# Attention with two expert layers on one core: weights scaled in their own step, one preparation step per block product, sums in PSUM

## The chip, the cores and the metric

The kernel runs on one core of a Trainium2 chip. The metric is the device time of one execution, in microseconds; lower is better. Five engines matter here: PE (TensorE, matrix products into PSUM), DVE (VectorE), ACT (ScalarE), POOL (GpSimd) and SP, whose queue issues all transfers. Each engine works through its own instructions in order and waits for the others by semaphores.

## What is computed

```
scores = (q @ k^T) / 8, causal mask, softmax          # 2 batches, 12 heads, 448 tokens, 64 wide
x = attention output, 896 tokens x 768
h = x @ w_in; g = h where h>=1, 0 where h<=-1, else (h+1)^2/4; y = g @ w_out       # 768 -> 2048 -> 768
xn = y / rms(y) * rms_g
out = (silu(xn @ w_gate) * (xn @ w_val)) @ w_out2                                   # 768 -> 1536 -> 768
```

The weights arrive as 64-bit floats, two 32-bit words each.

## The kernel before

The tokens are held transposed, in two halves h of 448 columns, so that every matrix product is 128x128 weights times 128x448 tokens. Each operand is kept as a high part and a low part (fp32r), and each product is the sum of three: high·high, high·low, low·high.

**Weights.** Each weight block, 128x768, is one item of a list. Its 768 KB are loaded into one of three stage buffers (`w_load`), and then steps turn the two words of a number into an fp32 value: `w_scale` (ACT, L167) multiplies the upper word, `w_low` (L169) calls it and has POOL make the low bits (L174), `w_high` (DVE, L185) joins both, and `parts` splits the value: ACT casts the high part (L193), POOL subtracts for the low part (L194). As soon as a stage buffer is read, `w_next` issues the next item's transfer into it. All these steps stand in one list; `w_run(n)` emits the next n of them at the place of the program where it is called, `w_pace(x)` emits 4x on average, `w_need(n)` all up to item n, and `w_cap` says how far they may run ahead. Every engine's order is thus the order in which the program emits, and nothing reorders it. `w_low(n)` scales item n and then item n+1 too:

```
    def w_low(n):
        w_scale(n)
        w_scale(n + 1)
```

**Stages.** Attention (to about 98 us), then the first expert layer (L363: w_in; L606 in `out1`: w_out, half h=0, then h=1), then the second. In `out1(1)` the sixteen blocks n are 18 products each; the four plain w_gate items and the first pair are prepared beside them. Then the sum of squares (`rms_sum`), the spread of the scale over the partitions (`rms_spread`, PE L665), and the token sums that a Strassen-like scheme needs: `normalise`, `mix` and `mix_late` make T1 to T4 and B22 out of the two halves (DVE L669, L734 to L743, ACT L674, POOL L675), beside the products `head` and `tail` of the first four gate blocks.

**Rounds.** For each of 12 blocks f a pair of items, w_gate[f] and w_val[f], is turned into sums of their 384-column halves, S1 to S4 (`combine_a`, `combine_b`: DVE L438 to L443), and block products `p1` to `p7` of nine matmuls each (L700) give the two outputs: five products per round for f<4, where `head` and `tail` did two, and seven from f=4 on. Pair f+1 is prepared in round f. Results leave PSUM by ACT copies (L769, L778, L790) or DVE additions (L710), and Silu (L797, L812) and products (L713) follow in SBUF. A pair takes ten steps, emitted at 1.44 or 2 per product.

**Last stage.** `out2` (L852): twelve w_out2 items, plain steps again, and 432 matmuls in two halves; ACT copies, and the output leaves.

## Time and profile before

| | us |
|---|---|
| median of 3 runs | 704.04 (703.42 to 704.18) |
| the profiled execution, its own time | 704.87 |
| its span in the profile | 703.2 |
| PE busy | 622.9 (89%) |
| ACT, DVE, POOL busy | 323.7, 315.5, 300.4 |
| mean granted TensorE clock | 0.937 |

PE's busy time counts matmuls at whatever clock was granted, so a stretch at half clock looks busy. The page's forty slices show PE full until the second third of the run and between six and nine tenths from there to the last weights; no other engine passes half of its time after attention. The views to read are therefore the busy time by stretch, the waits, and the timeline of the stretches where PE has gaps.

### The profile page before, as it was taken

The numbers are of one execution on the slowest core, as the hardware profiler recorded it, in microseconds if no ns is written. First come the engines' busy times: TensorE is split into PE (matmuls) and PEld (weight loads), VectorE is DVE, ScalarE is ACT, GpSimd is POOL, SyncE is SP. The second block draws the span as 40 slices with busy tenths as digits, with TensorE's granted clock in tenths as the row PEclk, the third lists the DMA queues.
The fourth block names the chain that finished last, engine by engine and source line by source line (L and its number), as shares of the span: only waits on it lengthen the run. The fifth ranks groups of instructions, "written<-read, shape, count | busy, mean of one in ns | idle before, by whom it ended". The sixth has DMA issues, their size and how long they took to land.

```text
span 703.2 us, 8626 instructions
## 1 busy us (share of the span) xinstructions
PE 622.9 (89%) x3236; PEld 529.3 (75%) x3236; DVE 315.5 (45%) x573; ACT 323.7 (46%) x636; POOL 300.4 (43%) x241
## 2 busy tenths in 40 slices
PE   7999999999999999998696576978788997888998
PEld 4666678999998997987584455867676876766997
DVE  5777742432333334233448554534444464425210
ACT  6887863666665443322235333333334443443311
POOL 3434422656554444225328444544444563554000
PEclk9999999999999999999888777888888899999999
DMA  8324210444543422012120222222222223441202
GB/s 291 126 86 132 99 59 1 135 170 149 176 155 115 134 91 89 1 46 90 57 79 0 90 90 89 90 89 90 90 90 79 102 89 106 162 137 45 80 1 79
DMA packets 17274, 68.19 MB, mean 97 GB/s; under 512 B 2064, under 2 KB 6672, under 8 KB 17232
## 3 DMA queue, kind: packets, MB, share of 16 engines
q1 hardware_dynamic: 17232, 67.64, 28.7%
q8 instruction: 25, 0.41, 0.2%
q14 instruction: 17, 0.14, 0.1%
HBM read 64.88 MB, written 2.75 MB: 96 GB/s over the span
## 4 chain that ended last, share of the span: by engine, by line
PE 47%; POOL 14%; issue 13%; DMA 11%; DVE 10%; ACT 5%; POOLq 0%; SPq 0%; ACTq 0%; DVEq 0%
PE ps L363 17%; POOL ar L194 10%; PE ps L852 8%; DMA af<-in_w_gate 8%; PE ps L269 5%; PE ps L606 4%; PE ps L300 4%; PE ps L700 4%; POOL af L174 4%; PE ps L348 3%; DVE af L185 3%; DMA af<-in_w_out 2%; ACT af L167 1%; PE ps L334 1%; DVE af L442 1%
## 5 line engine op out<-in xcount | busy, mean ns | idle before, releaser
L194 POOL TENSOR_TENSOR ar<-af,ar 128x768 fp32r<-128x768 f32 (+1 forms) x92 | 164.3, 1791 | 236.5 <-ACT ar L193 229.2
L700 PE MATMUL ps<-ar 128*128 128x448 f32 x756 | 186.0, 410 | 49.9 <-DVE af L710 20.2
L700 PEld LDWEIGHTS ps<-ar 128*128 128x128 f32 x756 | 159.9, 215 | 75.0 <-DVE af L710 23.2
L606 PE MATMUL ps<-ar 128*128 128x448 f32 x576 | 127.0, 380 | 10.7 <-ACT ar L566 7.2
L606 PEld LDWEIGHTS ps<-ar 128*128 128x128 f32 x576 | 111.6, 195 | 25.3 <-ACT ar L566 9.4
L363 PE MATMUL ps<-ar 128*128 128x448 f32 x576 | 117.6, 366 | 0.0
L167 ACT ACTIVATE af<-af 128x768 f32<-128x768 f32 x66 | 59.8, 907 | 120.7 <-DMA af<-in_w_gate 78.3
L363 PEld LDWEIGHTS ps<-ar 128*128 128x128 f32 x576 | 108.0, 188 | 8.6
L193 ACT CAST ar<-af 128x768 fp32r<-128x768 f32 (+1 forms) x92 | 74.4, 818 | 84.2 <-DVE af L185 76.9
L185 DVE SCALAR_TENSOR_TENSOR af<-af 128x768 int32<-128x768 int32 x72 | 68.6, 955 | 74.3 <-POOL af L174 74.1
L852 PE MATMUL ps<-ar 128*128 128x448 f32 x432 | 93.2, 374 | 9.4 <-DVE ar L836 5.1
L852 PEld LDWEIGHTS ps<-ar 128*128 128x128 f32 x432 | 81.8, 191 | 20.8 <-DVE ar L836 7.6
L174 POOL TENSOR_SCALAR af<-af 128x768 int32<-128x768 uint8 x72 | 67.8, 942 | 14.7 <-DMA af<-in_w_out 5.2
L567 DVE TENSOR_TENSOR ar<-af,ar 128x448 fp32r<-128x448 f32 x32 | 28.4, 893 | 73.8 <-ACT ar L566 73.8
L284 ACT ACTIVATE af<-ps,nm 112x336 f32<-112x336 f32 (+2 forms) x96 | 46.9, 500 | 7.1 <-DVE nm L276 7.1
L710 DVE TENSOR_TENSOR af<-ps,af 128x448 f32<-128x448 f32 x44 | 26.7, 621 | 50.8 <-PE ps L700 50.6
L276 DVE CUSTOM_DVE_ANT_0 ps<-ps,af 112x336 f32<-112x336 f32 (+2 forms) x96 | 41.6, 473 | 13.7 <-PE ps L269 12.6
L836 DVE TENSOR_TENSOR ar<-af,ar 128x448 fp32r<-128x448 f32 x24 | 20.7, 874 | 57.7 <-ACT ar L835 57.7
L713 DVE TENSOR_TENSOR af<-af 128x448 f32<-128x448 f32 x24 | 23.6, 985 | 40.7 <-ACT af L812 32.3
L269 PE MATMUL ps<-af 64*112 64x448 f32 (+3 forms) x192 | 35.5, 448 | 4.9 <-DVE af L247 4.7
L675 POOL TENSOR_TENSOR ar<-af,ar 128x448 fp32r<-128x448 f32 x18 | 23.8, 1339 | 27.5 <-ACT ar L674 27.4
L566 ACT CAST ar<-af 128x448 fp32r<-128x448 f32 x32 | 17.7, 563 | 29.8 <-PE ps L606 29.8
(72 smaller groups left out, 476.8 us busy)
## 6 DMA issues: line engine op xcount, KB each, us to landing
af<-in_w_out SPq DMA_DIRECT2D x28, 768.0 KB, 4.3
af<-in_w_in SPq DMA_DIRECT2D x16, 768.0 KB, 4.3
af<-in_w_gate SPq DMA_DIRECT2D x16, 768.0 KB, 4.2
af<-in_w_val SPq DMA_DIRECT2D x12, 768.0 KB, 4.3
af<-in_kT SPq DMA_DIRECT2D x12, 224.0 KB, 2.7
af<-in_qT SPq DMA_DIRECT2D x12, 224.0 KB, 3.3
af<-in_v SPq DMA_DIRECT2D x12, 224.0 KB, 2.6
out_T<-af SPq DMA_DIRECT2D x12, 224.0 KB, 1.9
```

Of the source, the lines that this page charges most:

```text
L167: nc.scalar.activation(c, c, ACTF.Prelu, scale=2.0 ** -112, alpha=-2.0 ** 32)
L174: nc.gpsimd.tensor_scalar(out=words(n, 0, I32), in0=b, scalar1=1.0 / 32, scalar2=-31.0 / 64, op0=ALU.mult, op1=ALU.add)
L185: nc.vector.scalar_tensor_tensor(out=t if raw is None else raw.bitcast(I32), in0=words(n, 1, I32), scalar=3, in1=t, op0=ALU.logical_shift_ ...
L193: nc.scalar.copy(hi, src)
L194: nc.gpsimd.tensor_tensor(out=lo, in0=src, in1=b32(hi), op=ALU.subtract)
L269: nc.tensor.matmul(bs[j][:C, o:o + (c + 1) * C], lhsT=q[r, c * C:(c + 1) * C], rhs=k[r, :(c + 1) * C], start=True, stop=True, skip_group_c ...
L276: nc.vector.tensor_tensor_reduce(out=t, in0=t, in1=mask[:C, S - (c + 1) * C:], scale=-1.0, scalar=3e38, op0=ALU.add, op1=ALU.min, accum_ou ...
L284: nc.scalar.activation(Pn[:C, j, poff[c]:poff[c] + w], sbank[n][j][:C, o:o + w], ACTF.Exp, bias=nm[:C, j, c:c + 1], scale=-1.0, accum_out= ...
L363: nc.tensor.matmul(out, lhsT=w[:, a, k * P:(k + 1) * P], rhs=x[:, c, k], start=(k == 0 and n == 0), stop=(k == NK - 1 and n == 2))
L606: nc.tensor.matmul(ybs[dm][:, :S], lhsT=w[:, a, dm * P:(dm + 1) * P], rhs=t[:, c], start=(n == 0 and i == 0), stop=(n == NM - 1 and i == 2))
L700: nc.tensor.matmul(b[:, :S], lhsT=w(a, k), rhs=x[:, c, k], start=first and k == 0 and i == 0, stop=(k == HK - 1 and i == 2), skip_group_ch ...
L852: nc.tensor.matmul(obs[dm][:, :S], lhsT=w[:, a, dm * P:(dm + 1) * P], rhs=t[:, c], start=(kk == 0 and i == 0), stop=(kk == NF - 1 and i == 2))
```

## The change

- `w_low(n)` scales the next item only where that item is marked early: w_in, w_out, and w_out2 after its first. The w_gate and w_val items are scaled in their own `w_low`.
- A pair now has seven steps: `gate_low`; `gate_high` (which also does the val item's `w_low`); `val_high` (with the parts of the gate block); `sums_a`; `sums_b`; `parts_a`; `parts_b`. One is emitted per product from f=4 on (`w_run(1)`), seven among five products for f<4; the second pair's first two are emitted among `head` and `tail`.
- From the second pair on, the val half v1 and the sums s1, s2 lie in PSUM banks 5, 6 and 7; the low parts of s1 and s2 are then made by DVE.
- `squares` scales by rms_g on ACT instead of DVE; for h=1 the sum of squares is made by DVE, in PSUM.
- The normalised tokens, one token sum (t2) and the results z and y of `p4` and `p3` lie in PSUM; T2 and B22 get their low part from DVE, T1, T3, T4 from POOL. `mix_a` begins before `tail(0)`.
- All PSUM banks are fixed by number.

The core of the diff:

```diff
     def w_low(n):
         w_scale(n)
-        w_scale(n + 1)
+        if n + 1 < len(items) and items[n + 1][2]:
+            w_scale(n + 1)
...
     def pair_steps(n, f):
         bl = block(f)
...
+        g1, g2 = rawg[:, :KP], rawg[:, KP:]
+        v1, s1, s2 = (bank(i)[:, :KP] for i in (5, 6, 7)) if f else (rawv[:, :KP], sraw[:, 2], sraw[:, 3])
+        v2, s3, s4 = rawv[:, KP:], sraw[:, 0], sraw[:, 1]
+        s12 = pst[:, 6:8, :KP] if f else sraw[:, 2:4]
...
+        def gate_low():
+            w_low(n)
+        def gate_high():
+            w_high(n, rawg)
+            w_next(n)
+            w_low(n + 1)
+        def val_high():
             if f >= NA:
                 parts(bl[:, 0, 5:7], bl[:, 1, 5:7], rawg.rearrange("p (a b) -> p a b", a=2))
+            w_high(n + 1, v1, v2)
+            w_next(n + 1)
+        def sums_a():
+            tt(s1, v1, v2, ALU.add)
+            tt(s3, g1, v1, ALU.subtract)
+        def sums_b():
+            tt(s2, s1, g1, ALU.subtract)
+            tt(s4, g2, s2, ALU.subtract)
+            parts(bl[:, 0, 4], bl[:, 1, 4], v2)
+        def parts_a():
+            nc.scalar.copy(bl[:, 0, 0:2], s12)
+            tt(bl[:, 1, 0:2], s12, b32(bl[:, 0, 0:2]), ALU.subtract)
+        def parts_b():
+            parts(bl[:, 0, 2:4], bl[:, 1, 2:4], sraw[:, 0:2])
...
+        return [gate_low], [gate_high, val_high, sums_a, sums_b, parts_a, parts_b]
...
+        def mix_a(i):
+            x0 = XF[0]
+            normalise(1, i, XA[i])
+            normalise(1, i + HK, XB[i])
+            xt = XF[1][i]
+            sub(xt, XA[i], x0[i])
+            sub(t2, XB[i], xt)
+            operand(T1, i, xt)
+            operand(T2, i, t2, nc.vector)
+        def mix_b(i):
+            x0 = XF[0]
+            sub(x0[i], t2, x0[i])
+            sub(x0[i + HK], x0[i + HK], t2)
+            operand(T3, i, x0[i])
+            operand(B22, i, XB[i], nc.vector)
+            operand(T4, i, x0[i + HK])
...
+        yb = [bank(f % 2) for f in range(NF)]
+        zb = [bank(2 + f % 2) for f in range(NF)]
+        cb = bank(4)
...
         def p4(f):
+            z = zb[f][:, :S]
             product(zb[f], op(f, A22), T4, first=False)
-            add(TMP[f][0], zb.pop(f), TMP[f][0])
-            mul(A[f][0], A[f][0], TMP[f][0])
+            add(z, zb[f], TMP[f][0])
+            mul(A[f][0], z, A[f][0])
...
             if f < NA:
-                run = [(p6, f), (p4, f - 1), (p7, f), (p5, f), (p3, f - 1)]
+                m = f < 2
+                run = [(p4, f - 1, 2), (p6, f, 2), (p7, f, 1), (p5, f, int(m)), (p3, f - 1, 2 - m)]
+            else:
+                run = [(p1, f, 1), (p4, f - 1, 1), (p6, f, 1), (p3, f - 1, 1), (p7, f, 1), (p5, f, 1), (p2, f, 1)]
+            for p, g, n in run:
                 if g >= 0:
                     p(g)
-                w_pace(0.36 if f >= NA else 0.5)
+                w_run(n if f < NF - 1 else 2)
```

The instructions, one by one, stand now as follows at three places. First ACT in one round from f=4 on. Before (L769, L778, L790: copies of `p1`, `p6`, `p5`; L812, L797: Silu; L167: scale; L193: parts):

```order
L769 COPY af<-ps 128x448
L167 ACTIVATE af<-af 128x768
L193 CAST ar<-af 128x768
L778 COPY af<-ps 128x448
L167 ACTIVATE af<-af 128x768
L812 ACTIVATE af<-ps 128x448
L790 COPY af<-ps 128x448
L193 CAST ar<-af 128x384
L797 ACTIVATE af<-af 128x448
L193 CAST ar<-af 128x768 x2
```

Now (L805, L812, L823: the copies; L842, L829: Silu; L475: the high part of s1 and s2; L200: the other parts):

```order
L805 COPY af<-ps 128x448
L167 ACTIVATE af<-af 128x768 x2
L812 COPY af<-ps 128x448
L200 CAST ar<-af 128x768
L842 ACTIVATE ps<-ps 128x448
L200 CAST ar<-af 128x384
L823 COPY af<-ps 128x448
L475 CAST ar<-ps 128x768
L829 ACTIVATE af<-af 128x448
L200 CAST ar<-af 128x768
```

Both scales now stand together behind the copy of `p1`; before, one scale (of the next pair's gate item) stood ahead of Silu and of the copy of `p5`.

Second, POOL in one round. Before (L174: low bits; L194: low parts):

```order
L174 TENSOR_SCALAR af<-af 128x768
L194 TENSOR_TENSOR ar<-af,ar 128x768
L174 TENSOR_SCALAR af<-af 128x768
L194 TENSOR_TENSOR ar<-af,ar 128x384
L194 TENSOR_TENSOR ar<-af,ar 128x768 x2
L174 TENSOR_SCALAR af<-af 128x768
```

Now (L175 and L201 are the same lines):

```order
L175 TENSOR_SCALAR af<-af 128x768 x2
L201 TENSOR_TENSOR ar<-af,ar 128x768
L201 TENSOR_TENSOR ar<-af,ar 128x384
L201 TENSOR_TENSOR ar<-af,ar 128x768
L175 TENSOR_SCALAR af<-af 128x768 x2
```

The gate's parts moved behind the second low bits, and one of the two 128x768 low parts at the end went to DVE.

Third, ACT in the last stage, two items. Before (L835: the tokens' high part, L193: the weights' high part, L167: scale):

```order
L835 CAST ar<-af 128x448
L193 CAST ar<-af 128x768
L167 ACTIVATE af<-af 128x768
L835 CAST ar<-af 128x448
L193 CAST ar<-af 128x768
L167 ACTIVATE af<-af 128x768
```

Now (L867 is the tokens' line):

```order
L167 ACTIVATE af<-af 128x768
L200 CAST ar<-af 128x768
L867 CAST ar<-af 128x448
L167 ACTIVATE af<-af 128x768
L200 CAST ar<-af 128x768
L867 CAST ar<-af 128x448
```

The tokens' cast moved from behind a scale and ahead of a high part to behind the high part.

## Rows read from the trace of the kernel before

**Rows 1.** Busy times by stretch: span, PE, PEld, DVE, ACT, POOL (instructions), clock, DMA share, GB/s

```profile
360.00:405.00 45.00, 27.96 (x107) 23.42 (x107) 28.70 (x39) 18.37 (x34) 24.07 (x19) 0.76 0.10 35
405.00:451.00 46.00, 36.41 (x136) 31.16 (x137) 23.51 (x35) 13.32 (x20) 21.61 (x17) 0.78 0.28 91
451.00:574.00 123.00, 102.88 (x444) 90.40 (x443) 59.33 (x79) 47.33 (x76) 60.66 (x43) 0.89 0.26 88
```

**Rows 2.** Waits, whole run: who waited for whom, us in total, times, longest us

```profile
...
ACT af L167 <- DMA af<-in_w_gate: 78.3, 15, 9.5
...
PE ps L700 <- DVE af L710: 20.2, 7, 4.2
...
```

**Rows 3.** Timeline, L606 stage to spread: start us, us, instruction, count, [idle before <-releaser]

```profile
...
269.49 0.88 ACT L167 ACTIVATE af<-af 128x768 f32<-128x768 f32 x1 [5.25 <-DMA af<-in_w_gate]
...
274.09 23.26 PE L606 MATMUL ps<-ar 128*128 128x448 f32 x104 [1.49 <-DVE ar L567]
...
306.12 3.96 PE L606 MATMUL ps<-ar 128*128 128x448 f32 x18
309.50 0.88 ACT L167 ACTIVATE af<-af 128x768 f32<-128x768 f32 x1 [6.22 <-DMA af<-in_w_gate]
...
346.56 0.88 ACT L167 ACTIVATE af<-af 128x768 f32<-128x768 f32 x1 [6.75 <-DMA af<-in_w_val]
...
347.94 10.22 PE L606 MATMUL ps<-ar 128*128 128x448 f32 x36 [3.90 <-ACT ar L566]
...
364.18 1.89 PE L665 MATMUL ps<-ident,rr 112*128 112x112 f32 x8
```

**Rows 4.** Timeline, the rounds of the second expert layer

```profile
471.16 15.24 PE L700 MATMUL ps<-ar 128*128 128x448 f32 x63 [4.20 <-DVE af L710]
...
555.82 0.91 ACT L167 ACTIVATE af<-af 128x768 f32<-128x768 f32 x1 [3.06 <-DMA af<-in_w_gate]
...
576.72 2.10 PE L700 MATMUL ps<-ar 128*128 128x448 f32 x9 [1.00 <-DVE af L710]
```

**Rows 5.** Timeline, last weights' low parts on POOL and PE's last stretch

```profile
578.62 1.83 POOL L194 TENSOR_TENSOR ar<-af,ar 128x768 fp32r<-128x768 f32 x1 [0.23 <-ACT ar L193]
...
593.66 1.87 POOL L194 TENSOR_TENSOR ar<-af,ar 128x768 fp32r<-128x768 f32 x1 [2.00 <-ACT ar L193]
...
641.04 1.88 POOL L194 TENSOR_TENSOR ar<-af,ar 128x768 fp32r<-128x768 f32 x1 [2.34 <-ACT ar L193]
...
648.54 51.14 PE L852 MATMUL ps<-ar 128*128 128x448 f32 x251 [1.17 <-DVE ar L836]
```

**Rows 6.** Groups by shape: line, operation, count, busy us, mean ns, idle before

```profile
L710 DVE TENSOR_TENSOR af<-ps,af 128x448 f32<-128x448 f32 x44 | 26.7, 621 | 50.8 <-PE ps L700 50.6
...
L641 DVE TENSOR_TENSOR af<-af 128x448 f32<-128x448 f32 x1 | 0.6, 624 | 0.0
...
L438 DVE TENSOR_TENSOR af<-af 128x384 f32<-128x384 f32 x12 | 6.7, 558 | 0.4
...
L442 DVE TENSOR_TENSOR af<-af 128x384 f32<-128x384 f32 x12 | 13.2, 1099 | 0.0
...
L185 DVE SCALAR_TENSOR_TENSOR af<-af 128x768 int32<-128x768 int32 x26 | 24.7, 954 | 14.5 <-POOL af L174 14.5
...
L167 ACT ACTIVATE af<-af 128x768 f32<-128x768 f32 x26 | 23.6, 910 | 64.1 <-DMA af<-in_w_gate 56.2 <-DMA af<-in_w_out 7.9
...
L193 ACT CAST ar<-af 128x768 fp32r<-128x768 f32 x35 | 28.4, 833 | 39.1 <-DVE af L185 31.8 <-DVE af L442 6.9 <-DVE af L443 0.4
...
L769 ACT COPY af<-ps 128x448 f32<-128x448 f32 x8 | 4.2, 522 | 0.0
...
L797 ACT ACTIVATE af<-af 128x448 f32<-128x448 f32 x8 | 4.6, 577 | 16.2 <-DVE af L710 16.2
...
L194 POOL TENSOR_TENSOR ar<-af,ar 128x768 fp32r<-128x768 f32 x35 | 64.5, 1853 | 50.0 <-ACT ar L193 50.0
...
L276 DVE CUSTOM_DVE_ANT_0 ps<-ps,af 112x448 f32<-112x448 f32 x24 | 14.6, 647 | 6.0 <-PE ps L269 5.9
```

More of the change, by code (lines that the diff above doesn't have):

```diff
@@ L180, in w_sign, with w_high @@
             nc.vector.scalar_tensor_tensor(out=c, in0=c, scalar=-2.0 ** 32, in1=c, op0=ALU.mult, op1=ALU.max)
[L182 to L190 removed]
+    def w_high(n, *outs):
+        if not outs:
+            outs = (value(n),)
+            if not wide:
+                return
+        o = 0
+        for out in outs:
+            c = slice(o, o + out.shape[-1])
+            o += out.shape[-1]
+            if wide:
+                nc.vector.scalar_tensor_tensor(out=out.bitcast(I32), in0=words(n, 1, I32)[:, c], scalar=3,
+                                               in1=words(n, 0, I32)[:, c], op0=ALU.logical_shift_left,
+                                               op1=ALU.bitwise_or)
+            else:
+                nc.vector.tensor_copy(out, value(n)[:, c])
     def parts(hi, lo, src):
@@ L479 @@
     for kk in range(NF):
[L480 removed]
+        plain(w_out2[kk * P:(kk + 1) * P], AR.at(W2_AT[kk], 2, NK * P), (2, 0, 1)[kk % 3], kk > 0)
     for w in work:
@@ L600, in out1 @@
         def out1(h, after, finish):
-            ybs = [nbank() for _ in range(NK)]
+            ybs = [bank((NK * h + i) % 8) for i in range(NK)]
             def mm(dm, n, t):
@@ L632 @@
         ACC = [a_slot(2), a_slot(26)]
+        RB = [bank(4), bank(7)]
+        ysum = bank(5)[:, :S]
         def squares(h):
```

142 lines of the change are left out of this document (51 added, 91 removed).

## The prediction

> **What bounds the kernel now.** I read the busy times by stretch first, because a share over the whole run mixes stages. From 360 to 574 us no engine but PE is busy half of the time, except DVE at 28.7 of 45.0 us in the first stretch, and yet PE has 167 of 214 us, at a granted clock of 0.76 to 0.89 [rows 1]. A matmul takes 51.14/251 = 0.2037 us where PE runs without a gap [rows 5]; 107, 136 and 444 matmuls would be 140 us. So some 74 us of the 214 are gaps and slow clock. The waits say who ends the gaps: ACT stood 78.3 us, in 15 waits, before the scale L167 for a w_gate transfer, and PE stood for L710, a DVE addition, which waits for an ACT copy [rows 2]. The timeline shows the link. In the L606 stage the scale of the next item stands on ACT ahead of the cast that PE needs; it waits 5 to 7 us for a transfer issued just before, and PE stops (3.90 us before 347.94) [rows 3]. In the rounds it stands ahead of Silu and of the copy of `p5`; DVE's addition to `p5` comes late, and `p4` of the next round, which writes the same bank, waits 4.20 us for it [rows 4]. In the last stage the bound is another: one item's low part follows the last one's every (641.04 - 593.66)/9 = 5.26 us, while its products take 18 x 0.2037 = 3.67 us [rows 5].
>
> The sum is made against the profiled execution: span 703.2, own time 704.87, so 1.7 us lie around the span. It is 0.8 us above the median of 704.04. Less than about 0.2% cannot be told from no change here.
>
> **L606 stage.** Removed from ACT's way: the waiting scales of the four w_gate items and of the first pair. A plain item's scale now comes four steps, at 0.42 x 4 = 1.68 steps per block more than two blocks or 7.3 us, after its transfer was issued; the profile's list of transfers has 4.2 us to landing for w_gate. What is left is the first val item: its transfer starts when the last gate item's low part ends, and its scale stands one block later. I count its wait at about 4 us on ACT, of which 1.9 reach PE, since the cast behind it belongs to the block after next. From 306.12 there are 10 blocks, 180 matmuls, 36.7 us, so PE could be through at 342.8; it ended at 347.94 + 10.22 = 358.2 [rows 3]. Of 15.4 us lost, 13.5 return. Earlier, the gap before 274.09 (1.5) and 104 matmuls in 23.26 instead of 21.2 us return 3.6. From the last block to the end of the spread (366.1) it stays near 8 us: ACT now has 12 operations of 0.54 instead of 6, but DVE, not POOL, adds the squares. Together 17.1; I take **16**, between 10 (the val wait shows in full) and 19.
>
> **Token sums and the first four rounds.** DVE's work per index of the token sums is 2 normalisations, 4 sums and 2 low parts, 8 operations, all with one PSUM operand. None of the trace's rows shows a plain DVE addition that writes PSUM. The nearest are L710, 0.621 us with one operand read from PSUM; L641, 0.624 with both in SBUF; L276, which reads and writes PSUM, 0.647 for 448 columns [rows 6]. I take 0.62, the price of L710, and keep 0.55 and 1.2 (twice L710) as ends. Two waits per index for ACT's casts add 1.1: 8 x 0.62 + 1.1 = 6.1, three times 18.3, plus one `w_high` of 0.95 (L185). Then DVE has the val halves and two sums of the second pair (4 x 0.56, the price of L438 [rows 6]), the addition to `p6`, two more sums, one 768-column low part (0.95, from the slope between L438 and L710) and two additions: 6.2. `p4(0)` starts 25.3 us after the spread. PE has its eight `head` and `tail` products under this.
>
> In rounds 1 to 3 DVE has per round 7 additions and products (4.3), `w_high` of both items (0.95 + 1.1), four sums (2.2), the low part (0.95) and one wait for Silu (0.7): 10.3 us; PE has 45 x 0.2037 = 9.2. DVE bounds these rounds. Three rounds, and `p1(4)`, which waits for the last product that reads its bank, end in `p4(3)` at 59.1 and, with one round of 13.1 from below, `p4(4)` at 72 us after the spread. Before, it was 471.16 - 366.07 = 105.1 [rows 3, 4]: **33** us come back, between 22 and 38. Two things did it: the waits for transfers, and that DVE's sums with both operands in SBUF took 1.10 in L442 where the same shape took 0.56 in L438 [rows 6]; with an operand in PSUM, L710 never varied so.
>
> [...]
>
> **Rounds from f=4 on.** Seven products are 63 x 0.2037 = 12.8 us. Per round DVE has 5 additions and products (3.1), 2.1 of `w_high`, 2.2 of sums, 0.95: 8.4. ACT has two scales (1.8), three copies (1.6), three casts of 768 columns (2.5), one of 384 (0.5), two Silu (1.2): 7.6. POOL has two low parts of 1.85, half of one more and two low bits, some 7. All fit below PE [rows 6]. The transfers are issued six steps, some 11 us, before their scale, so landing is covered; without that cover each round pays up to 4.5 us. What is late next is a chain across the round's end: `p2` ends, DVE adds (0.6, behind the 768-column low part that ends 0.6 us after `p2`), Silu 0.6, the high part of s3 and s4 0.8, the copy of `p1` 0.5 (L797, L193, L769). It ends 3.1 us after `p2`; `p6` starts 3.7 after it. So the slack is 0.5 us, and I allow 0.27 per round: 13.1 us. The six rounds between 471.16 and 576.72 took 105.6 [rows 4]; six of 13.1 are 78.6: **27** us, between 18 and 29.
>
> **Last stage.** The last pair's low part ended at 580.45, 3.7 us after `p4(10)` began; now I count 2.6, as its steps spread evenly. From there nothing is shortened but the order on ACT: the tokens' cast no longer stands between a scale and the next high part. The chain low bits, `w_high`, high part, low part (0.9 to 1.15, 0.95, 0.83, 1.85 and the steps between) is about 5.06 instead of 5.26 us, 2 us in eleven items. PE reaches the items earlier but must still wait for the last low part, so only **3** us, between 0 and 7, are won. Transfers and products removed: none.
>
> **The sum**: 16 + 33 + 27 + 3 = 79. The span becomes 624.2, the time 625.9: **626 us**.
>
> **Rivals.**
> - *PSUM destinations cost DVE twice.* For: no row shows one. Against: L276. Nine more writes in the token sums (5.4) and five per round in three rounds (9.0) cost 14 us; from f=4 on DVE stays at 10.8, below PE. 640 us.
> - *The chain from `p2` to the copy of `p1` holds the rounds.* For: 0.5 us of slack, on three engines. Against: each link is short and nothing else is ahead of it. At 2 us per round, eight rounds with the tail, 642 us.
> - *The scales still wait.* The change would not do what it says: two transfers in flight beside the casts, and ACT stands before L167 in every round as in the row of 555.82 (3.06 us) [rows 4]. For: rounds 1 to 3 read 1.5 MB in 10 us. Against: the lead of six steps. The L606 stage would return 9 instead of 16, and 2 us per round would stay in eleven rounds: 655 us at the worst.
> - *Slower*: DVE becomes the bound in all rounds. Its twelve operations with PSUM in a round, and one `w_high`, would have to fill today's round of 105.6/6 = 17.6 us: (17.6 - 0.95)/12 = 1.4 us each, 2.2 times L710. From there on every 0.1 us more costs 1.2 us per round. At 1.6 us the rounds are 20.2, 2.6 more than now; eight of them lose 21 us, the token sums win nothing, and with 10 won in the L606 stage the time is about 715. For it speaks only that every one of these operands shares PSUM with the running products; against it L710, 0.621 over 44 runs while PE writes other banks.
>
> **How the numbers follow.** The forecast (612 to 636) has 0.64, DVE's doubled writes 0.12, the chain 0.13, the waiting scales 0.07, the slower case 0.04. The low end takes the good ends of the terms in part: 3 more from the L606 stage, 3 from the token sums, 3 from rounds without any allowance, 4 at the end: about 612. The high end, 652, holds each of the first two rivals whole (640, 642) and most of both together (656). All cases but the last are faster by far more than 0.2%: 0.95 faster, 0.01 same, 0.04 slower.
>
> **What would show it.** ACT's waits for w_gate transfers fall from 78 us to below 15. `p4` to `p4` is 12.8 to 13.4 us from f=4 on, with granted clock 1.0 there; rounds 1 to 3 are 10 to 11 us with DVE over 90% busy. Plain additions that write PSUM read 0.6 to 0.7 us. The last stage still shows low parts 5.0 to 5.2 us apart, and PE waiting for them: that becomes the next bound. The prediction is wrong if PE waits in the rounds for the copy of `p1`, if a PSUM write takes over 0.9 us, or if the low parts of the last stage come further apart than 5.3 us.

## The result and the profile after

The changed kernel takes 640.21 us (median of 4 runs, 638.73 to 642.79) against 704.07: ratio 0.9099, 95% interval 0.9068 to 0.9129. The forecast was 626, the range 612 to 652. The profiled execution took 638.73 us, its span is 637.0, its mean granted clock 0.981 instead of 0.937. Line numbers have moved: L606 is now L632, L665 is L693, L700 is L728, L710 is L738, L185 is L193, L194 is L201, L769 is L805, L778 is L812, L852 is L884, L836 is L868.

First the busy times of two stretches of the page's windows view, in the columns of [rows 1]: the four rounds f=0 to 3 with the token sums, and the rounds from f=4 on.

```profile
349.00:426.00 77.00, 64.47 (x281) 54.73 (x280) 57.10 (x93) 35.99 (x59) 37.99 (x30) 0.91 0.31 103
426.00:508.00 82.00, 79.80 (x389) 72.37 (x388) 56.98 (x80) 41.99 (x66) 45.16 (x30) 1.00 0.34 116
```

From 426 to 508 us PE is busy 79.80 of 82 us at a granted clock of 1.00, where [rows 1] had 102.88 of 123 at 0.89. In the earlier stretch DVE is the busiest engine beside PE, as it was before (28.70 of 45.00 us in the first of [rows 1], more than the half said of the slices).

The waits of the whole run, in the columns of [rows 2]:

```profile
ACT af L167 <- DMA af<-in_w_out: 22.9, 19, 6.5
...
PE ps L884 <- DVE ar L868: 8.4, 7, 1.5
...
ACT af L167 <- DMA af<-in_w_val: 4.2, 1, 4.2
...
PE ps L728 <- ACT af L805: 2.7, 5, 0.6
```

The 78.3 us that ACT stood for w_gate [rows 2] have no row any more. What is left for w_val is one wait of 4.2 us; PE now waits a little for the copy of `p1` (L805) in the rounds, and for the tokens' low part (L868) in the last stage.

PE's timeline from the L632 stage on, which answers to [rows 3 to 5]:

```profile
334.23 0.47 PE L632 MATMUL ps<-ar 128*128 128x448 f32 x1 [2.04 <-ACT ar L592]
...
347.88 1.14 PE L693 MATMUL ps<-ident,rr 112*128 112x112 f32 x8
...
374.92 11.28 PE L728 MATMUL ps<-ar 128*128 128x448 f32 x54 [1.69 <-DVE af L738]
...
410.81 44.75 PE L728 MATMUL ps<-ar 128*128 128x448 f32 x207 [4.09 <-DVE af L741]
...
496.86 13.03 PE L728 MATMUL ps<-ar 128*128 128x448 f32 x63 [0.56 <-ACT af L805]
510.42 5.74 PE L728 MATMUL ps<-ar 128*128 128x448 f32 x27 [0.53 <-ACT af L805]
520.19 6.15 PE L728 MATMUL ps<-ar 128*128 128x448 f32 x18 [4.03 <-ACT af L812]
...
578.76 54.79 PE L884 MATMUL ps<-ar 128*128 128x448 f32 x269 [1.17 <-DVE ar L868]
```

The spread ends at 349.02 instead of 366.07. `p4(0)`, with which round 1 begins, starts at 374.92; `p1(4)` at 410.81 after a wait of 4.09; `p4(4)`, 72 matmuls later, at 427.80; `p4(10)`, the last nine of the group at 496.86, at 507.91. From `p4` to `p4` the six rounds take 12.77, 13.01, 13.58, 13.59, 13.56 and 13.59 us. Against the forecast, term by term:

| stretch | before | after | won | forecast |
|---|---|---|---|---|
| to the end of the spread | 366.1 | 349.0 | 17.1 | 16 |
| spread to `p4(4)` | 105.1 | 78.8 | 26.3 | 33 |
| six rounds, `p4(4)` to `p4(10)` | 105.6 | 80.1 | 25.5 | 27 |
| `p4(10)` to the end | 126.5 | 129.1 | -2.6 | 3 |
| span | 703.2 | 637.0 | 66.2 | 79 |

DVE's groups by shape from 349 to 580 us, in the columns of [rows 6]:

```profile
L193 DVE SCALAR_TENSOR_TENSOR af<-af 128x384 int32<-128x384 int32 x11 | 18.6, 1689 | 0.0
L738 DVE TENSOR_TENSOR af<-ps,af 128x448 f32<-128x448 f32 x28 | 17.3, 618 | 4.3 <-ACT af L823 4.2
...
L449 DVE TENSOR_TENSOR ps<-ps,af 128x384 f32<-128x384 f32 x22 | 12.2, 556 | 0.1
L449 DVE TENSOR_TENSOR af<-af,ps 128x384 f32<-128x384 f32 x22 | 12.1, 548 | 0.4
...
L738 DVE TENSOR_TENSOR ps<-ps,af 128x448 f32<-128x448 f32 x16 | 10.1, 630 | 21.2 <-PE ps L728 21.2
L193 DVE SCALAR_TENSOR_TENSOR ps<-af 128x384 int32<-128x384 int32 x11 | 6.3, 572 | 5.2 <-POOL af L175 5.2
```

A plain addition that reads and writes PSUM (L738) takes 630 ns, one that reads PSUM and writes SBUF 618. But the two halves of the val item's high part, the same operation on the same shape, take 572 and 1689 ns.

### The profile page after: what moved, and what is told of

Same layout as the page of the kernel before. It is cut to its first block, busy times and chain, and to the rows that moved or that the text cites. A ratio compares the mean times of both kernels' runs of the same rounds, so it can differ in the third digit from the quotient of the medians.

```text
span 637.0 us, 8655 instructions
## 1 busy us (share of the span) xinstructions
PE 592.3 (93%) x3236; PEld 510.5 (80%) x3236; DVE 320.8 (50%) x592; ACT 331.2 (52%) x648; POOL 273.9 (43%) x222
## 4 chain that ended last, share of the span: by engine, by line
PE 61%; POOL 12%; DVE 11%; issue 10%; ACT 4%; DMA 2%; POOLq 0%; SPq 0%; ACTq 0%; DVEq 0%
PE ps L370 18%; PE ps L632 14%; PE ps L884 9%; POOL ar L201 6%; PE ps L276 5%; POOL af L175 5%; PE ps L728 5%; PE ps L307 4%; PE ps L355 4%; DVE af L193 3%; DVE af L449 2%; PE ps L341 2%; DVE ps L449 1%; DMA af<-in_w_out 1%; ACT ar L702 1%
## 5 line engine op out<-in xcount | busy, mean ns | idle before, releaser
L201 POOL TENSOR_TENSOR ar<-af,ar 128x768 fp32r<-128x768 f32 (+1 forms) x80 | 142.0, 1775 | 216.6 <-ACT ar L200 211.7
L728 PE MATMUL ps<-ar 128*128 128x448 f32 x756 | 167.8, 382 | 21.0 <-DVE af L738 5.3
L728 PEld LDWEIGHTS ps<-ar 128*128 128x128 f32 x756 | 146.8, 197 | 41.2 <-DVE af L738 7.8
L632 PE MATMUL ps<-ar 128*128 128x448 f32 x576 | 118.3, 366 | 2.4 <-ACT ar L592 2.0
L193 DVE SCALAR_TENSOR_TENSOR af<-af 128x768 int32<-128x768 int32 (+1 forms) x73 | 78.0, 1070 | 81.9 <-POOL af L175 81.7
L370 PE MATMUL ps<-ar 128*128 128x448 f32 x576 | 117.5, 366 | 0.0
L632 PEld LDWEIGHTS ps<-ar 128*128 128x128 f32 x576 | 107.9, 188 | 12.0 <-ACT ar L592 2.4
L370 PEld LDWEIGHTS ps<-ar 128*128 128x128 f32 x576 | 108.0, 188 | 8.6
L200 ACT CAST ar<-af 128x768 fp32r<-128x768 f32 (+1 forms) x80 | 65.6, 819 | 81.8 <-DVE af L193 81.7
L884 PE MATMUL ps<-ar 128*128 128x448 f32 x432 | 89.9, 368 | 10.0 <-DVE ar L868 8.4
L884 PEld LDWEIGHTS ps<-ar 128*128 128x128 f32 x432 | 80.5, 188 | 19.5 <-DVE ar L868 11.2
L175 POOL TENSOR_SCALAR af<-af 128x768 int32<-128x768 uint8 x72 | 73.4, 1019 | 14.4 <-DMA af<-in_w_out 5.1
L167 ACT ACTIVATE af<-af 128x768 f32<-128x768 f32 x66 | 58.6, 905 | 35.4 <-DMA af<-in_w_out 22.9
L593 DVE TENSOR_TENSOR ar<-af,ar 128x448 fp32r<-128x448 f32 x32 | 27.5, 864 | 67.4 <-ACT ar L592 67.4
L868 DVE TENSOR_TENSOR ar<-af,ar 128x448 fp32r<-128x448 f32 x24 | 27.0, 1140 | 45.9 <-ACT ar L867 45.9
L383 DVE SCALAR_TENSOR_TENSOR af<-af,ps 128x448 f32<-128x448 f32 x32 | 19.3, 616 | 26.1 <-ACT af L379 26.1
L378 ACT ACTIVATE af<-ps,half 128x448 f32<-128x448 f32 x32 | 20.1, 629 | 20.8 <-PE ps L370 20.8
L307 PE MATMUL ps<-ident,af 112*112 112x112 f32 x240 | 30.6, 266 | 0.0
```

Of the source, the lines that this page charges most:

```text
L167: nc.scalar.activation(c, c, ACTF.Prelu, scale=2.0 ** -112, alpha=-2.0 ** 32)
L175: nc.gpsimd.tensor_scalar(out=words(n, 0, I32), in0=b, scalar1=1.0 / 32, scalar2=-31.0 / 64, op0=ALU.mult, op1=ALU.add)
L193: nc.vector.scalar_tensor_tensor(out=out.bitcast(I32), in0=words(n, 1, I32)[:, c], scalar=3, in1=words(n, 0, I32)[:, c], op0=ALU.logical_s ...
L200: nc.scalar.copy(hi, src)
L201: nc.gpsimd.tensor_tensor(out=lo, in0=src, in1=b32(hi), op=ALU.subtract)
L307: nc.tensor.transpose(bs[j][:C, o:o + C], Pn[:C, j, poff[c] + kc * C:poff[c] + (kc + 1) * C], ident[:C, :C])
```

## The experiments

Each profile is cut at the same three events of PE: the end of the spread, the start of `p1(4)`, and the end of `p7(11)`, 54 products or 486 matmuls later. For the changed kernel that is 349.0, then 410.8 - 349.0 = 61.8, then 510.42 + 5.74 - 410.81 = 105.4, and 120.8 to the end of the span. "Ratio" is to the kernel before on the same chip, with its 95% interval; E2 is a variant of the kernel before, whose order differs, and stands in the text alone.

| | time, us | ratio | spread ends | to `p1(4)` | 486 matmuls | rest |
|---|---|---|---|---|---|---|
| changed kernel | 640.21 | 0.9099 [0.9068, 0.9129] | 349.0 | 61.8 | 105.4 | 120.8 |
| E1 scales in front again | 689.51 | 0.9806 [0.9774, 0.9838] | 371.3 | 67.3 | 128.4 | 121.1 |
| E3 token sums in SBUF | 646.58 | 0.9199 [0.9165, 0.9233] | 349.7 | 67.3 | 105.3 | 122.2 |
| E4 rounds' sums in SBUF | 645.58 | 0.9183 [0.9147, 0.9220] | 351.2 | 64.0 | 108.0 | 120.6 |
| E5 steps in twos | 647.91 | 0.9194 [0.9164, 0.9223] | 353.1 | 61.8 | 110.2 | 121.1 |
| E6 gate low part later | 636.77 | 0.9059 [0.9029, 0.9089] | 351.8 | 62.8 | 102.2 | 119.6 |
| E7 split first | 637.60 | 0.9070 [0.9042, 0.9099] | 349.9 | 61.7 | 105.3 | 118.8 |
| E8 both | 633.75 | 0.9024 [0.8976, 0.9073] | 349.2 | 61.7 | 102.2 | 116.4 |
| E9 last items overlapped | 627.68 | 0.8923 [0.8880, 0.8967] | 349.6 | 61.8 | 100.3 | 110.5 |
| E10 high part ahead of split | 623.76 | 0.8853 [0.8823, 0.8883] | 348.8 | 61.8 | 102.2 | 106.7 |
| E11 additions ahead of sums | 624.54 | 0.8861 [0.8833, 0.8889] | 350.1 | 59.7 | 101.8 | 111.2 |
| E12 and gate low part early | 621.69 | 0.8842 [0.8819, 0.8865] | 353.6 | 59.7 | 101.1 | 108.8 |

All four parts belong to one execution each. The spread's end moves by up to 5 us from E3 to E12 with one transfer, and the 486 matmuls by 2 us with PE's own pace, both told at the end; the rest moves with the first w_out2 transfer, for which ACT stood 5.80 us in E10 and E12, 6.50 in the changed kernel and 8.00 in E11. So a part is read from the column that its edit touches.

**E1, the scales back in front.** In the changed kernel:

```diff
     def w_low(n):
         w_scale(n)
-        if n + 1 < len(items) and items[n + 1][2]:
-            w_scale(n + 1)
+        w_scale(n + 1)
```

> The changed kernel with the scale put back: every item's scale is again issued in the cast step of the item before it, right behind the issue of its transfer, as the kernel before did it; sums in PSUM and the preparation step per block product stay. Theory A (the scale's waits for transfers cost 13 to 17 us in the L606 stage of the kernel before, and 2 to 4 us in rounds): ACT waits again for w_gate transfers, 60 us or more in all, the spread ends at 358 to 366 us instead of 349, rounds from f=4 on are 14 to 17 us, and the time is 660 to 690. Rival B (with sums in PSUM and evenly spread steps the waits mostly lie beside other work): the L606 stage loses 10 to 17 us, rounds stay within 0.5 us of 13.57, the time is 650 to 658. Rival C (the evenly spread steps alone hide the wait): under 645.

The time is 689.51 us. Theory A has the direction and, at its edge, the time; its rounds (14 to 17 us) and its spread (358 to 366) were still too mild. Its lines stand one lower (L811 is the copy of `p6`). Its waits, then the timeline of ACT and PE:

```profile
ACT af L167 <- DMA af<-in_w_gate: 99.7, 15, 7.8
```

```profile
484.06 0.88 ACT L167 ACTIVATE af<-af 128x768 f32<-128x768 f32 x1 [7.32 <-DMA af<-in_w_gate]
...
485.40 15.97 PE L727 MATMUL ps<-ar 128*128 128x448 f32 x63 [2.88 <-ACT af L811]
504.45 14.80 PE L727 MATMUL ps<-ar 128*128 128x448 f32 x63 [3.07 <-ACT af L811]
```

At 484, 503 and 521 us ACT has stood 7.3 to 7.8 us before a scale, PE waits 2.9 to 3.1 us for an ACT copy behind it, and the second group shown begins 19.05 us behind the first. The groups of the first five rounds begin 17.2 to 19.1 us apart. The whole loss, 22.3 + 5.5 + 23.0 us, lies in the three stretches in which w_gate items are prepared; the last stage, whose items keep their early scale, is unchanged.

**E2, the scale's own step alone, in the kernel before.** The same test in `w_low`, with w_in, w_out and w_out2 (but its first) marked early, and nothing else of the change:

```diff
     def w_low(n):
         w_scale(n)
-        w_scale(n + 1)
+        if n + 1 < len(items) and items[n + 1][2]:
+            w_scale(n + 1)
...
-        items.append((w_in[m], wslot(m), None))
+        items.append((w_in[m], wslot(m), True))
```

> The kernel before with one part of the change alone: every plain item, val item and last weight has its scale in a step of its own, well behind the issue of its transfer; the order of the steps, the sums in SBUF and the tokens' sums stay as before. From putting the scale back into the changed kernel, which cost 49 us, theory A: the scale is the larger part by itself too, ACT no longer waits for w_gate transfers (78.3 us before, below 15 here), the spread ends at 349 to 352 us instead of 366, rounds fall to 14.5 to 16.5 us, the time is 655 to 675. Rival B (the parts only work together: with unevenly spread steps and the slower sums, another wait takes the place of the scale's): the spread ends 15 to 18 us earlier, rounds stay at 17 us or more, the time is 683 to 690.

667.68 us, ratio 0.9506 [0.9465, 0.9546]: theory A. No wait for w_gate is left; the spread ends at 345.0, earlier than A's 349 to 352 and 4 us earlier than in the changed kernel, and rounds are 14.5 to 16.4 us (lines one higher than before: L701 the products, L711 the additions, L770 the copy of `p1`):

```profile
445.24 11.92 PE L701 MATMUL ps<-ar 128*128 128x448 f32 x54 [0.92 <-ACT af L770]
...
461.65 11.93 PE L701 MATMUL ps<-ar 128*128 128x448 f32 x54 [0.94 <-ACT af L770]
```

So the scale is worth 702.4 - 667.7 = 34.7 us by itself and 49 us on top of the rest; the rest is worth 13.8 us without it (E1) and 27.5 with it. Neither part can be priced alone: as long as ACT stands for a transfer, faster sums lengthen the wait (for w_gate 99.7 us in E1, 78.3 before [rows 2]).

**E3, the tokens' sums in SBUF.**

```diff
-        XA = [bank(i % 2)[:, :S] for i in range(HK)]
-        XB = [bank(2 + i % 2)[:, :S] for i in range(HK)]
-        t2 = ysum
+        XA = [XF[1][i] for i in range(HK)]
+        XB = [XF[1][i + HK] for i in range(HK)]
+        t2 = a_slot(16)
```

> The changed kernel with one part undone: the tokens' sums and differences between the spread and the first rounds lie in SBUF, not in PSUM; the order of the operations is that of the changed kernel. Theory A (DVE's operations with both operands in SBUF are held up while POOL runs a two-operand low part): the sums and differences of 448 columns rise from 0.63 to a mean of 0.8 to 1.2 us, the first product of the first round comes 27 to 33 us after the spread instead of 25.9, the time is 642 to 648. Rival B (POOL has too little to do there, so where the sums lie does not matter): the mean stays at 0.62 to 0.66, the first product comes 25 to 26.5 us after the spread, the time stays within 1.5 us of 640.2.

646.58 us: theory A in time (642 to 648) and at the start of the first round: `p4(0)` begins 379.81 - 349.65 = 30.2 us after the spread instead of 25.9. But not by the operations it named. DVE's groups, same window:

```profile
L758 DVE TENSOR_TENSOR af<-af 128x448 f32<-128x448 f32 x12 | 7.7, 661 | 0.1
L703 DVE TENSOR_TENSOR ar<-af,ar 128x448 fp32r<-128x448 f32 x6 | 6.5, 1082 | 3.6 <-ACT ar L702 3.6
```

The sums are at 661 ns, below the 0.8 to 1.2 us expected; the low parts L703, which read the sum and its high part, both now in SBUF, went from 625 to 1082. POOL makes its own low parts of T1, T3 and T4 (L703 too, 1300 ns) just then.

**E4, the rounds' sums in SBUF.**

```diff
-        v1, s1, s2 = (bank(i)[:, :KP] for i in (5, 6, 7)) if f else (rawv[:, :KP], sraw[:, 2], sraw[:, 3])
+        v1, s1, s2 = (bank(i)[:, :KP] for i in (5, 6, 7)) if False else (rawv[:, :KP], sraw[:, 2], sraw[:, 3])
-        s12 = pst[:, 6:8, :KP] if f else sraw[:, 2:4]
+        s12 = pst[:, 6:8, :KP] if False else sraw[:, 2:4]
```

> The changed kernel with one part undone: sums of the weights' halves in the rounds (v1, s1, s2 and the wide low part of s3 and s4's source) stay in SBUF for every pair, as the first pair has them; token sums stay in PSUM. Theory A (DVE additions with both operands in SBUF are stretched by POOL's parts to about 1.0 to 1.1 us, and an operand in PSUM avoids it): the sums of 384 columns rise from 0.56 to 0.8 to 1.1 us, four per round, the chain from p2 to the copy of p1 is 1 to 2.5 us longer, rounds are 14.5 to 16 us instead of 13.57, the time is 650 to 664. Rival B (where the sums lie matters little, since DVE has room in the rounds): rounds stay within 0.3 us of 13.57 and the time within 4 us of 640.2.

645.58 us, between the theories: the later rounds are 13.97 us instead of 13.57, below A's 14.5 and above B's 13.87. The two views, DVE's groups and PE's timeline:

```profile
L449 DVE TENSOR_TENSOR af<-af 128x384 f32<-128x384 f32 x44 | 31.0, 743 | 0.5
```

```profile
475.54 13.03 PE L728 MATMUL ps<-ar 128*128 128x448 f32 x63 [0.95 <-ACT af L805]
489.51 13.03 PE L728 MATMUL ps<-ar 128*128 128x448 f32 x63 [0.94 <-ACT af L805]
```

Four sums lose 0.19 us each on average, and half of that reaches the copy of `p1`. PSUM's share of the gain is thus about 5 us here and 6 in E3.

**E5, the steps in twos.**

```diff
-                run = [(p1, f, 1), (p4, f - 1, 1), (p6, f, 1), (p3, f - 1, 1), (p7, f, 1), (p5, f, 1), (p2, f, 1)]
+                run = [(p1, f, 2), (p4, f - 1, 0), (p6, f, 2), (p3, f - 1, 0), (p7, f, 2), (p5, f, 0), (p2, f, 1)]
```

> The changed kernel with its rounds from f=4 on given the preparation steps in twos (two after p1, two after p6, two after p7, one after p2) instead of one after each product; scales, sums in PSUM and all else stay. Theory A (even steps matter by themselves: in twos, some 2 us of preparation stand on DVE and ACT ahead of an addition or a copy on the chain that ends at the copy of p1): the wait in front of the 63 products rises from 0.55 us to 1.2 to 3 us, the time is 644 to 660. Rival B (once the scales no longer wait, the engines have room and the order is of no weight): rounds of 13.3 to 13.9 us, the time within 3 us of 640.2.

647.91 us; 4.8 us of it in the 486 matmuls, some 4 in the stretch to the spread, which the edit does not touch. The time fits A, by luck of that stretch; without the 4 us it would stand near A's lower edge. The place does not fit: the wait for the copy of `p1` fell to 0.2 us, and a new one, 0.93 us for a DVE addition, stands ahead of each round's last product. DVE's timeline in one round:

```profile
480.58 2.10 DVE L193 SCALAR_TENSOR_TENSOR ps<-af 128x384 int32<-128x384 int32 x1
482.59 0.55 DVE L193 SCALAR_TENSOR_TENSOR af<-af 128x384 int32<-128x384 int32 x1
```

and POOL's:

```profile
480.41 1.84 POOL L201 TENSOR_TENSOR ar<-af,ar 128x768 fp32r<-128x768 f32 x1 [0.19 <-ACT ar L200]
```

Here the half that is written to PSUM is the long one, because it now is the one that meets POOL. So the destination is not what counts.

**E6, the gate block's low part later.** That collision, moved away in the changed kernel:

```diff
         def val_high():
-            if f >= NA:
-                parts(bl[:, 0, 5:7], bl[:, 1, 5:7], rawg.rearrange("p (a b) -> p a b", a=2))
             w_high(n + 1, v1, v2)
...
         def sums_a():
             tt(s1, v1, v2, ALU.add)
             tt(s3, g1, v1, ALU.subtract)
+            if f >= NA:
+                parts(bl[:, 0, 5:7], bl[:, 1, 5:7], rawg.rearrange("p (a b) -> p a b", a=2))
```

> The changed kernel with one step moved: the gate block's low part (and low bits) of POOL is issued at the end of the first step of the sums instead of at the start of the val halves, so that it no longer stands beside DVE's second half of the high part of v2. Theory A (POOL's two-operand work beside DVE's two-operand work on SBUF stretches the half from about 0.57 to 2.2 us, and this makes p6 wait 0.53 to 0.56 us for the copy of p1 in every round): the 384-column half falls from a mean of 1.51 us to below 0.8, the wait in front of the 63 products falls to below 0.2, rounds are 12.9 to 13.1 us instead of 13.57, round 3 (first with gate parts) gains 1 to 2 us; the time is 4 to 7 us below 640.2, about 634.5. Rival B (the half is long for its own operands' sake; the wait comes from elsewhere on the chain from p2): the half stays above 1.4 us, rounds stay at 13.5 to 13.6, the time stays within 1.5 us of 640.2. Rival C (POOL's part moved only meets another DVE operation, the sums with an operand in PSUM or the next high part): the half falls but some other DVE operation lengthens by 0.5 us or more and rounds gain less than 0.2 us.

636.77 us, 3.4 less than the changed kernel and not A's 4 to 7. The interval overlaps that of the changed kernel; the trace settles it (DVE's group from 410 to 525 us, then PE):

```profile
L193 DVE SCALAR_TENSOR_TENSOR af<-af 128x384 int32<-128x384 int32 x7 | 3.9, 552 | 0.0
```

```profile
414.57 102.20 PE L728 MATMUL ps<-ar 128*128 128x448 f32 x486 [4.09 <-DVE af L741]
```

The half takes 0.55 us, no wait for the copy of `p1` is left, and the 486 matmuls stand in one group: theory A in its cause. The clock fell behind the 4.09 us stop (0.62 to 418 us, 0.89 to 422); from `p4(4)` on every round is 13.02 us, within A's 12.9 to 13.1. The sums that now stand beside POOL keep 0.55 to 0.56 us, so rival C falls too. Its 1 to 2 us in round 3 did not come: there ACT and POOL stand idle when the step is issued, so they start as early as before, and the half beside them still takes 2.20 us. A later place in the program moved the instruction only where its engine had a queue.

**E7, the tokens' split first** (last stage):

```diff
             for kk in range(NF - late):
+                split2(h * NF + kk + 3)
                 if h == 0:
                     w_need(W2_FIRST + kk + 1)
                     w_cap[0] = len(items)
                     w_pace(1)
-                split2(h * NF + kk + 3)
```

> The changed kernel with one call moved: in the last stage the tokens' split is emitted ahead of the four steps of the item, where the kernel before had it in effect one block earlier. Theory A (the last stage takes longer than predicted because the tokens' low part comes behind the item's steps on DVE and ACT, so that PE runs one block late): the wait of PE for the tokens' low part in front of each block goes, after the last item's low part about 251 products are left instead of 269, the stage is 3 to 4 us shorter, the time about 636.5. Rival B (the bound is the period of the items' low parts on POOL, and the order of the split only shifts where PE waits): the products left after the last item stay at 269 or the time stays within 1 us of 640.2. Beyond that: if the split ahead delays the item's own high part on DVE or ACT, low parts come further apart than 5.1 us and up to 2 us are lost again.

637.60 us: theory A, but 2.6 us instead of its 3 to 4, and again with overlapping intervals. 251 matmuls are left behind the last item instead of 269, but that item comes 0.5 us later, counted from `p1(4)`, and PE's pace is slower in this execution (52.13 us for the 251, where the kernel before took 51.14 [rows 5]).

```profile
580.11 52.13 PE L884 MATMUL ps<-ar 128*128 128x448 f32 x251 [1.18 <-DVE ar L868]
```

**E8, both moves.** The two diffs above together.

> The changed kernel with both moved steps of the two runs before: the gate block's low part behind the sums, and the tokens' split ahead of the item's steps in the last stage. Apart they gave 3.4 and 2.6 us (636.77 and 637.60 against 640.21). Theory A (they lie in different stages and add up): 633.5 to 635.5. Rival B (what the rounds win is waited away in the last stage, whose start hangs on transfers or on the item chain rather than on PE): 636 to 637.5.

633.75 us (631.28 to 638.03): they add up, 102.2 us in the rounds and 116.4 in the rest.

**E9, the last items overlapped.** E8, with the last stage's steps rearranged: POOL's low bits of item n+1 ahead of the low part of item n, the scale of n+1 behind the cast of n.

```diff
+    def w2_steps(n):
+        def a():
...
+            w_high(n)
+        def b():
+            if n + 1 < len(items):
+                w_bits(n + 1)
+        def c():
+            w_cast(n)
+            w_scale(n + 1)
+        return [a, b, c, lambda: w_sub(n)]
```

> Both moved steps, and the last stage's preparation overlapped: POOL takes the low bits of item n+1 ahead of the low part of item n, and ACT scales item n+1 right behind the high part of item n. Theory A (the last stage is bound by one item's chain of low bits, high part on DVE, cast on ACT and low part on POOL, 5.08 us, and not by an engine: POOL has 3.2 us of work per item, the products 18 x 0.2037 = 3.67): low parts come 3.7 to 4.2 us apart, PE runs the 432 products of the stage nearly without a gap (88 to 92 us instead of 96.4), the time is 626 to 631. Rival B (transfers or DVE, whose high part waits while POOL runs a low part, set the pace): low parts 4.6 us apart or more, the time is 632 to 636.

627.68 us, within A's time; but the low parts come 4.94 us apart, which is B's number. B's reason is only a part of it: beside POOL the high part takes 1.62 us instead of 0.96, but the wait stands elsewhere. DVE's timeline:

```profile
543.47 1.62 DVE L193 SCALAR_TENSOR_TENSOR af<-af 128x768 int32<-128x768 int32 x1
547.34 1.15 DVE L902 TENSOR_TENSOR ar<-af,ar 128x448 fp32r<-128x448 f32 x1 [2.24 <-ACT ar L901]
548.40 1.62 DVE L193 SCALAR_TENSOR_TENSOR af<-af 128x768 int32<-128x768 int32 x1
```

The next high part stands behind the tokens' low part L902, which waits for ACT's cast L901, which ACT reaches only behind cast and scale of the item. What is won comes chiefly from the first items: from the first low part to the fourth it is 11.1 us (514.23 to 525.33), in E8 14.9 (515.38 to 530.30).

**E10, the high part ahead of the split.** ACT's cast of the tokens stays ahead of the item's steps, DVE's low part goes behind the high part.

```diff
             w_high(n)
+            split_low()
...
-                split2(h * NF + kk + 3)
+                split_cast(h * NF + kk + 3)
...
                     w_pace(1)
+                split_low()
```

> The kernel of the run with overlapped last items (627.68 us, low parts 4.94 us apart instead of the expected 3.7 to 4.2), with one call divided: ACT's cast of the tokens' split still comes ahead of the item's steps, but DVE's low part of the tokens now comes behind the item's high part. Theory A (the 4.94 us are one ring: high part 1.62, its cast 0.90, the next scale 0.8, the tokens' cast 0.55, the tokens' low part 1.15, and only then the next high part, because DVE takes its operations in order): the ring is broken, low parts come 3.2 to 4.2 us apart, PE runs the 432 products of the last stage in 88 to 90 us instead of 92.2, the time is 623 to 626. Rival B (the pace is set by DVE's high part being held up beside POOL, or by the transfers): low parts stay 4.7 us apart or more, the time stays within 1.5 us of 627.7.

623.76 us (621.26 to 626.25): theory A. POOL's low parts come 543.12, 546.84, 550.97, 554.68, 558.47, or 3.8 us apart, although the high part takes 1.9 to 2.3 us beside POOL, so that B's reason falls. PE does the last stage without a gap (L930 its products, L527 the tokens' low part):

```profile
528.45 87.62 PE L930 MATMUL ps<-ar 128*128 128x448 f32 x431 [0.70 <-DVE ar L527]
```

87.62/431 = 0.2033 us per matmul: this stage now goes at PE's own pace.

**E11, DVE's additions ahead of the sums in the round f=3.** To E10:

```diff
                 run = [(p4, f - 1, 2), (p6, f, 2), (p7, f, 1), (p5, f, int(m)), (p3, f - 1, 2 - m)]
+                if f == NA - 1:
+                    run = [(p4, f - 1, 2), (p6, f, 0), (p7, f, 1), (p5, f, 0), (p3, f - 1, 4)]
```

> The kernel of the run before this one, with the steps of the fourth round (f=3) put later: the high part of the val block comes after p7 and the sums and parts of the pair of f=4 behind p3, so that DVE's additions to p5 and p3, for which p1 of f=4 waits 4.0 to 4.1 us, stand ahead of them, and the gate block's low part on POOL no longer meets the second half of the high part there (2.20 us in that round). Theory A (the wait is only DVE's order, as DVE is idle for 4.5 us right after): the wait in front of p1(4) falls to 1.5 to 2.5 us, at most 1 us of it comes back as a wait for s2 in front of p6(4), the time is 1 to 2.5 us below the run before. Rival B (the sums come late for p6(4) by as much as p1(4) comes early): within 0.8 us of the run before.

624.54 us, rival B in time, but for another reason than B's (L770 are the rounds' products):

```profile
409.84 0.65 PE L770 MATMUL ps<-ar 128*128 128x448 f32 x2 [2.04 <-ACT ar L200]
411.73 99.92 PE L770 MATMUL ps<-ar 128*128 128x448 f32 x484 [1.24 <-POOL ar L201]
```

`p1(4)` is ready 2.1 us earlier after the spread (59.7 instead of 61.8), and after two matmuls it stops for POOL: it also reads the gate block's low part, which the same edit had put behind Silu. I had overlooked that reader. The stop of 1.24 us takes back most: `p4(4)` stands 77.5 us after the spread, in E10 78.3. That the time is not lower at all lies in the rest, 4.5 us longer in this execution, 2.2 of them in ACT's wait for the first w_out2 transfer; that the edit causes this is not shown.

**E12, that one low part back.**

```diff
         def val_high():
+            if f == NA:
+                parts(bl[:, 0, 5:7], bl[:, 1, 5:7], rawg.rearrange("p (a b) -> p a b", a=2))
...
-            if f >= NA:
+            if f > NA:
```

> The kernel with DVE's additions of the fourth round ahead of the sums (624.54 us), but the gate block's part of that one pair back at the start of the val halves; all later pairs keep it behind the sums. Theory A (what the additions won there, p1(4) ready 5.95 us after p3 of that round began instead of 8.0, was lost again because p1(4) also reads the gate block's low part, which ACT and POOL now made 1.2 to 1.9 us too late): p1(4) starts 5.9 to 6.3 us after that p3, without a second wait for POOL, p6(4) waits at most 1 us for s2, and the time is 1 to 2.5 us below 623.76, about 622. Rival B (POOL's low part beside the val halves holds DVE, and with it the additions, as long as before): p1(4) starts 7.5 to 8.1 us after that p3, the time is within 1 us of 623.8.

621.69 us (620.25 to 624.87), theory A: `p1(4)` starts 413.34 - 407.41 = 5.93 us after `p3` began, and no second wait follows (L772 are the products).

```profile
407.41 3.98 PE L772 MATMUL ps<-ar 128*128 128x448 f32 x18 [0.64 <-DVE af L782]
413.34 101.11 PE L772 MATMUL ps<-ar 128*128 128x448 f32 x486 [1.95 <-DVE af L785]
```

Its interval overlaps E10's, so that the gain of the last step is shown by the trace alone: `p4(4)` stands 74.9 us after the spread, in E10 78.3. Against the changed kernel this version is 18 us faster.

## Why the prediction was right, and where it was not

**L606 stage, right, with some luck.** 16 forecast, 17.1 measured; the one wait foreseen, 1.9 us for the first val item's scale, stands there with 2.04. E1 and E2 show that the scale's place is the cause. In E3 to E12, the same kernel up to here, the spread ends at 348.8 to 353.6, so that 12 to 17 us are won. In E2, with the old order of steps, no wait of PE over 0.2 us stands before the last products, so that the wait of 2.04 belongs to the change's own order of steps.

**The price of PSUM, right.** DVE's additions with a PSUM destination cost 0.63 us against 0.62 [rows 6], and the first rival falls. Reading from PSUM cost them no more either: 618 ns with one operand there, where L641 took 624 with both in SBUF [rows 6].

**Token sums and first rounds, 7 us too good.** `p4(0)` came 25.9 us after the spread (25.3 forecast), `p1(4)` 61.8 (57.3, nine matmuls before 59.1), `p4(4)` 78.8 (72). The step that failed is DVE's sum for rounds 1 to 3, in two terms. `w_high` of both items was priced at 0.95 + 1.1, from a row of whole items [rows 6], but in round 3 the gate block's low part of the pair of f=4 begins on POOL, and DVE's second half took 2.20 instead of 0.55. And DVE's wait for POOL's low bits ahead of `w_high` was put at nothing; in round 2 it stood 1.82 + 0.24 us for them, in round 3 1.47 + 0.26. Its timeline, the first wait of each round:

```profile
389.70 0.96 DVE L193 SCALAR_TENSOR_TENSOR af<-af 128x768 int32<-128x768 int32 x1 [1.82 <-POOL af L175]
...
401.26 0.96 DVE L193 SCALAR_TENSOR_TENSOR af<-af 128x768 int32<-128x768 int32 x1 [1.47 <-POOL af L175]
```

`p1(4)` waited 4.09 us for the DVE product behind all this and the sums. E12 got 2.1 us of that back by order; no run takes the waits for the low bits away, so their share is read from the trace alone. Nor was DVE over 90% busy there, but 27.70 of 36 us from 375 to 411. Some 2 us more lie behind the stop, where the granted clock read 0.85 from 410.81 to 427.80: 72 matmuls took 17.0 us instead of 14.7.

**Rounds from f=4 on, 1.5 us too good.** The first two rounds took 12.8 and 13.0 us, the other four 13.6 instead of 13.1. The named chain across the round's end does hold those four, as the second rival said, but with 0.53 to 0.56 us, not with 2; so the wait for the copy of `p1`, which the prediction named as a sign of being wrong, is there. The slack of 0.5 us was used up by the same half, 1.65 us too long in each round from f=5 on; E6 took that away and the wait was gone. The failed term is again the price of `w_high`, taken without asking what POOL does in that moment, where the rows of L442 beside L438, 1099 and 558 ns [rows 6], had shown that this matters: eight of the twelve L442 began during a low part on POOL and took 1.35 to 1.51 us, the others 0.55.

**Last stage, wrong in sign.** The step that failed is that PE only has to wait for the last low part, so that what the items win is won. The low parts do come closer, (576.35 - 540.72)/7 = 5.09 us, between 5.0 and 5.2 as said, and the last one begins 68.4 us after `p4(10)` instead of 69.4. But the order shown in front, the tokens' cast behind the item's high part, was counted only as a relief for ACT; on the way to PE it puts the tokens' low part one block late, and 269 matmuls instead of 251 are left behind the last item, 18 x 0.2037 = 3.7 us. E7 shows it. There too DVE meets POOL: the tokens' low part begins beside each item's and takes 1.92 to 1.95 us, before mostly 0.63 to 0.98; what this costs no run shows.

That the last item came 1 us earlier, and not 3, has two reasons in the trace. The step of 5.26 us [rows 5] is a mean with one step of 5.96 in it; the others were 5.17. And the last pair's low part ended 3.9 us after `p4(10)`, not 2.6. The wait that the change removes is also left here in one place: ACT stands for the first w_out2 transfer ahead of the copy of `p6(11)` (L812), and PE waits 4.03 us for that copy (520.19 above):

```profile
516.87 1.71 ACT L167 ACTIVATE af<-af 128x768 f32<-128x768 f32 x2 [6.50 <-DMA af<-in_w_out]
```

The forecast's 79 us became 66.2: 17.1 + 26.3 + 25.5 - 2.6, rounded. The slower rival needed DVE at 1.4 us per operation with a PSUM operand; it is at 0.62.

## What to carry to other kernels

Put a step that waits for a transfer well behind the transfer's issue and behind nothing that another engine is waiting for; its price is that of all that is queued behind it, and other improvements show little until it is gone. Price an operation by what the neighbouring engine does at that moment, not by its mean: for DVE beside POOL, see whether both inputs come from SBUF (0.55 us alone and 2.20 beside POOL for the half here). When an order changes, follow each operand to its last reader, and ask for each moved instruction whether its engine has a queue at all.
